# Two zero fills of the output moved behind the last token gather, with the expert weights one slot earlier

## The chip, the cores and the metric

The kernel runs on one core of a Trainium2 chip. The core has five engines: TensorE (PE: matmuls and weight loads), VectorE (DVE), ScalarE (ACT), GpSimd (POOL) and the sync engine (SP), which here only issues transfers. Transfers between DRAM and on-chip memory run on 16 DMA engines that all queues share: those that SP or ACT issue (queue q1 and q10 in the profile) and those that Pool issues (queue q0, which can also convert types and use indices). The metric is the device time of one execution in microseconds (us). The profile counts the span from the first to the last instruction, which is about 2 us shorter.

## The reference

Sparse attention is followed by a layer of experts with a capacity. There are 4 batches, 8 heads, 768 positions and 64 elements a head; 8 experts of 512 x 1024 x 512, each of which takes at most 80 tokens.

```python
# attention: each query keeps the 6 best chunks of 32 keys (by an upper bound), causal
ub = np.sum(np.maximum(q[..., None, :] * k_min[:, :, None], q[..., None, :] * k_max[:, :, None]), axis=-1)
top_chunks = np.argsort(np.where(causal, ub, -1e9), axis=-1)[..., -6:]
...
attn_out = softmax(masked scores) @ v
x = attn_out.transpose(0, 2, 1, 3).reshape(3072, 512)
# experts
logits = x @ w_gate;  expert_idx = argmax(logits);  gate_w = softmax(logits)[expert_idx]
out = np.zeros((3072, 512), dtype=np.float32)
for e in range(8):
    tok_idx = tokens of expert e, of which at most 80 with the largest gate_w
    h = np.maximum(x[tok_idx] @ w1[e], 0.0)
    out[tok_idx] = gate_w[tok_idx, None] * (h @ w2[e])
```

(The lines in words stand for code that is cut.) At most 640 of the 3072 rows of the output are not zero. So the kernel writes zeros over the whole output, 1536 KB for each of the four batches, and then scatters the rows of the experts into it. A row's scatter must come after the zeros of its batch, and since a round of rows may lie in any batch, each scatter waits for all four fills.

## The kernel before

The program is written with a helper, `op(engine, instruction, r=..., w=...)`. It works out from the names that an operation reads (`r`) and writes (`w`) which semaphores its engine must wait for. `sp` and `gpd` are transfers issued by SP and by Pool. Each engine runs its operations in program order.

The main loop runs over 16 pairs of heads, `i` = 0 to 15 (`NP` = 16); pair `i` belongs to batch `i // 4`. Weights are loaded meanwhile, one transfer of 1024 KB (as written, in bf16; the source is f32) at the end of a pair:

```python
def wload(e, part):          # part 0: w1 of expert e, part 1: w2
    ...
    op("gpd", lambda: gp.dma_start(w1s[e][:], src), w=[f"w1_{e}"], dsem=f"d_w1_{e}")
...
def fill(g, zs, zk):         # zeros over the output of batch g, from a zeroed tile
    zd = bass.AP(out.tensor, out.offset + g * NT * 128 * Dm, [[Dm, 128], [128 * Dm, NT], [1, Dm]])
    op("sp", lambda: sp.dma_start(zd, zs), r=[zk], w=[f"outz{g}"], dsem=f"d_zero{g}")

def last_w2(fbs):            # w2 of the last expert, in 8 pieces of 128 KB, into freed buffers
    for fb in fbs:
        ...
        op("gpd", lambda: gp.dma_start(w2f(E - 1, fb), src), ..., w=[f"w27{fb}"], dsem="d_w2_7")

for i in range(NP):
    ...
    if i == NP - 1:
        wload(E - 1, 0)
    folds(i, 0, 1)
    if i == NP - 1:
        last_w2(range(4))
    ...
    rows(i - 1); scale_rows(i - 1)        # writes the pair's rows to x_rows in DRAM (SP)
    ...                                   # at i == NP - 2: fill(3) from a cleared part of G
    if 0 < i < NP - 3:
        wload((i - 1) // 2, (i - 1) % 2)
    if i == NP - 2:
        wload(E - 2, 0)
        wload(E - 2, 1)
    if i in (0, 1, 12):                   # fills 0, 1, 2; the zeros lie in w1s[6], not loaded yet
        ...
        fill(min(i, 2), bass.AP(w1s[E - 2], ...), zk)
```

After the loop come the last pair's rows, the choice of tokens (`idx`, and per round the rows' places `idR` and weights `gR`), and the experts. A gather fetches an expert's tokens from `x_rows`, `turn` transposes them, `up` multiplies by w1 and applies Relu (first half on ACT, second half on DVE), and `down` multiplies by w2. There are six rounds of `down`, each over four groups of 32 rows. A round ends with an eviction on DVE, scaled, into one of four buffers `y`, and a scatter into the output:

```python
def gather(e):
    op("gpd", lambda: gp.indirect_dma_start(xgv(e), None, xd, ...),
        r=XD + ["idx"] + ([f"xS{e - 3}"] if e > 2 else []), w=[xgk(e)], dsem=f"d_g{e}")
...
def down(r):
    ...                                   # 32 matmuls into OB (the last round: 64, in two halves)
    op("dve", lambda: ve.tensor_scalar(yv(r)[:, c0:c1], o, gR[:, r:r + 1], None, ALU.mult),
       r=[k, "gR"], w=[f"y{r % 4}"] + k0)
    op("gpd", lambda: gp.indirect_dma_start(out, ..., yv(r), None, ...),
       r=[f"y{r % 4}", "idR"] + [f"outz{g}" for g in range(B)], w=[f"out{r}"], dsem=f"d_o{r % 4}")

for e in range(3):
    gather(e)
keep_warm(4); spread(); ...; keep_warm(12)       # idle matmuls while the gathers run
turn(0)
gather(3)
keep_warm(2)
up(0, lambda: turn(1, "dve"))
gather(4)
for e in range(1, E):
    if 1 < e + 1 < E:
        turn(e + 1)
        if e + 4 < E:
            gather(e + 4)
            if e + 4 == E - 1:
                last_w2(range(4, FB))
    up(e)
    if e % 4 > 0 and e != 3:
        down(e // 4 * 3 + e % 4 - 1)             # e = 1, 2, 5, 6, 7: rounds 0, 1, 3, 4, 5
    elif e == 4:
        down(2)
```

`xS{e - 3}` is the copy of the transposed tokens of expert e - 3, whose gather buffer is used again. Round 4 uses the buffer `y0` of round 0 again, and round 5 that of round 1.

Of the kernel before, what the change touches and what calls it, by code (L numbers as in the profile page):

```python
# [147 lines left out]
def bass_quest_chunk_select__then__topk_capacity_drop_kernel(  # L148
# [57 lines left out]
    with ExitStack() as pers:  # L206
# [17 lines left out]
        with nc.Block() as blk:  # L224

            @blk.sync
            def _body(_unused):
# [102 lines left out]
                def xgk(e):  # L330
                    return ("qn", "kn")[e % 2] + f"{e // 4}{e // 2 % 2}"
# [580 lines left out]
                    op("act", lambda: ac.activation(bass.AP({"q": qn, "k": kn}[n][s], 0, [[NT * 2 * D, CAP], [1, 512]]), zero, ACTF.Copy, scale=0.0),  # L912
                       r=[f"{n}n{s}{g}" for g in range(4)] + ["ident_f"], w=[f"{n}n{s}0", f"{n}n{s}1"])

                def fill(g, zs, zk):
                    zd = bass.AP(out.tensor, out.offset + g * NT * 128 * Dm, [[Dm, 128], [128 * Dm, NT], [1, Dm]])
                    op("sp", lambda: sp.dma_start(zd, zs), r=[zk], w=[f"outz{g}"], dsem=f"d_zero{g}")

                def last_w2(fbs):
                    for fb in fbs:  # L920
# [9 lines left out]
                for i in range(NP):  # L930
                    kk, bb = i % NPB, i // NPB - 1
                    live = bb >= 0
                    scores(i, 0, 2)
                    if i == NP - 1:
                        sort_rows(True)
                        vw_mm()
                        clear_xg("k", 0)
                    if i:
                        sums(i - 1)
                        scale_lg(i - 1)  # L940
                    if i == NP - 1:
                        wload(E - 1, 0)
                    folds(i, 0, 1)
                    if i == NP - 1:
                        last_w2(range(4))
                    if live and kk == 0:
                        gate_in(bb)
                    if live and kk == 1:
                        rank_pred()
                        rank_cmp(bb, 5)  # L950
                    scores(i, 2, 4)
                    if i == 0:
                        take_r(1)
                    if i == NP - 2:
                        op("act", lambda: ac.activation(G[:, 0:Dm], bass.AP(ident_f, 0, [[128, 128], [0, Dm]]), ACTF.Copy, scale=0.0),
                           r=["ident_f"], w=["growP"])
                    if live and kk == 2:
                        rank_count(bb)
                        rank_slot(bb)
                    if live and kk == 3 and i < NP - 1:  # L960
                        table(bb)
                        merge(bb)
                    if i == 12:
                        sort_apply()
                        sort_take()
                    if i:
                        if i == NP - 1:
                            sort_rank(0)
                        rows(i - 1)
                        scale_rows(i - 1)  # L970
                    if i == NP - 2:
                        fill(3, bass.AP(G, 0, [[2 * S, 128], [0, NT], [1, Dm]]), "growP")
                        rank_late(bb)
                    if live and kk == 0:
                        gate_exp()
                        gate(bb)
                    scores(i, 4, 6)
                    if i + 1 < NP:
                        bounds(i + 1)
                    if i + 2 < NP:  # L980
                        take_q(i + 2)
                        take_r(i + 2)
                    if i + 1 < NP:
                        bounds_out(i + 1)
                    if i + 2 < NP:
                        take_k(i + 2)
                    if i == 3:
                        op("dve", lambda: ve.tensor_scalar(triM[:], triQ[:], 1.0, 3e38, ALU.is_ge, ALU.mult), r=["triQ"], w=["triM"])
                        op("dve", lambda: ve.scalar_tensor_tensor(triM[:], ident_f[:], 3e38, triM[:], ALU.mult, ALU.max),
                           r=["triM", "ident_f"], w=["triM"])  # L990
                    if i + 4 < NP:
                        load(i + 4, "qk")
                    if i == NP - 4:
                        load_vk(NP - 1, 0)
                    if live and kk == 0:
                        rank_own(bb)
                    if live and kk == 1:
                        rank_diag(bb)
                        rank_cmp(bb, 4, 3, 2, 1, 0)
                    if live and kk == 2 and i < NP - 2:  # L1000
                        rank_late(bb)
                    if i == NP - 1:
                        sort_rank(1)
                        break
                    if i == NP - 2:
                        for n, s in (("q", 0), ("q", 1), ("k", 1)):
                            clear_xg(n, s)
                    values(i)
                    if i == NP - 2:
                        table(bb)  # L1010
                        merge(bb)
                        vw_turn()
                    if i + 2 < NP:
                        load(i + 2, "v")
                    if i + 1 < NP:
                        unselT(i + 1)
                    if live and kk == 0:
                        rank_row(bb)
                    if i == 11:
                        sort_rows(False)  # L1020
                        sort_rank()
                    if 0 < i < NP - 3:
                        wload((i - 1) // 2, (i - 1) % 2)
                    if i == NP - 2:
                        wload(E - 2, 0)
                        wload(E - 2, 1)
                    if i in (0, 1, 12):
                        zk = f"w1_{E - 2}"
                        zt = bass.AP(w1s[E - 2], 0, [[DB * Fd, 128], [1, 2 * Dm]]).bitcast(F32)
                        if i == 0:  # L1030
                            op("dve", lambda: ve.memset(zt, 0.0), w=[zk])
                        fill(min(i, 2), bass.AP(w1s[E - 2], 0, [[DB * Fd, 128], [0, NT], [1, 2 * Dm]]).bitcast(F32), zk)

                b = B - 1
                sums_last()
# [91 lines left out]
                def down(r):  # L1127
                    last = r == 5
                    groups = [(r // 3 * 4 + e, sb) for e, sb in ROUNDS[r % 3]]
                    o = OB[:, r % 2 * 512:r % 2 * 512 + Dm]  # L1130
                    parts = [(o, f"O{r % 2}", 0, Dm)]
                    if last:
                        n = Dm // 2
                        parts = [(o[:, 0:n], f"O{r % 2}", 0, n), (SC[0][:, 0:n], "SC0", n, Dm)]
                    for o, k, c0, c1 in parts:
                        for fb in range(FB):
                            for g, (e, sb) in enumerate(groups):
                                op("pe", lambda: pe.matmul(o[g * 32:g * 32 + 32, :], hTv(e)[:, fb * HW + sb * 32:fb * HW + sb * 32 + 32],  # L1138
                                                           w2f(e, fb)[:, c0:c1], start=(fb == 0), stop=(fb == FB - 1)),
                                   r=[f"hT{e % 4}{fb // 4}"] + ([f"w2_{e}"] if e < E - 1 else [f"w27{f}" for f in range(FB)]), w=[k], inc=(fb == FB - 1 and g == 3))  # L1140
                        k0 = ["E2", "E3", "E4", "E5"] if r == 0 else []
                        op("dve", lambda: ve.tensor_scalar(yv(r)[:, c0:c1], o, gR[:, r:r + 1], None, ALU.mult),
                           r=[k, "gR"], w=[f"y{r % 4}"] + k0)
                    op("gpd", lambda: gp.indirect_dma_start(
                        out, bass.IndirectOffsetOnAxis(ap=idR[:, r:r + 1], axis=0), yv(r), None,
                        bounds_check=NTOK - 1, oob_is_err=False), r=[f"y{r % 4}", "idR"] + [f"outz{g}" for g in range(B)], w=[f"out{r}"], dsem=f"d_o{r % 4}")

                for e in range(3):
                    gather(e)
                keep_warm(4)  # L1150
                spread()
                for e in range(4):
# [8 lines left out]
# [3 lines that stand above are left out]
                        if e + 4 < E:  # L1164
                            gather(e + 4)
                            if e + 4 == E - 1:
                                last_w2(range(4, FB))
                    up(e)
                    if e % 4 > 0 and e != 3:
                        down(e // 4 * 3 + e % 4 - 1)  # L1170
                    elif e == 4:
                        down(2)
# [36 lines left out]
```

## Time and profile before

| | |
|---|---|
| time, median of 3 runs | 290.12 us (290.0 to 290.32) |
| span of the profiled execution | 288.1 us |
| busy: PE, DVE, ACT, POOL | 274.3, 213.1, 147.0, 227.2 us |
| chain that ended last: PE, POOL, DVE, DMA | 70%, 15%, 6%, 4% of the span |
| three fills from `w1s`, one from `G` | 7.8 and 6.9 us from issue to landing (median of the page) |
| rows of a pair to `x_rows`, 16 transfers of 192 KB | 6.1 us median |
| w1 and w2 loads of 1024 KB | 9.8 and 11.2 us median |
| gathers, scatters | 2.6 us, 3.4 us median |

The page has the busy time of each engine, the span in 40 slices, the DMA queues, the chain of work that ended last (followed back from the last instruction through whatever released it), the costliest groups of instructions, and the transfers with their time from issue to landing. The trace behind it answers closer questions: single instructions in order of time, who waited for whom, and the share of the DMA engines in any stretch. A transfer's instruction on its queue is short; the transfer itself ends at its landing, when its semaphore is raised. A busy PE is no proof of progress, since the kernel also runs matmuls that only keep the array's clock up (`keep_warm`).

### The profile page before, as it was taken

To read this page: it belongs to the slowest core of one execution; us is meant where nothing else is said; L and a number is where in the kernel's file an instruction comes from. 1 tells how busy PE (TensorE), PEld (TensorE's weight loads), DVE (VectorE), ACT (ScalarE), POOL (GpSimd) and SP (SyncE) were. 2 spreads that over 40 slices of the span, in tenths; PEclk is the share of its full clock that TensorE was granted. 3 is DMA by queue.
4 is the path that set the end of the run, shared out by engine and by line. 5 is a ranking of instruction groups with operands and counts; after the bars stand their busy time and mean duration, and the time that the engine had idled before them with its cause. 6 is when DMAs were issued, how large, how long until landed. Compare 5 with 4: busy or idle time off the path is not lost.

```text
span 288.1 us, 8696 instructions
## 1 busy us (share of the span) xinstructions
PE 274.3 (95%) x3609; PEld 170.0 (59%) x3609; DVE 213.1 (74%) x575; ACT 147.0 (51%) x202; POOL 227.2 (79%) x295
## 2 busy tenths in 40 slices
PE   7899999999999999999999999999999999859991
PEld 7454656565656565656565656666656666428761
DVE  5897455566988989659889898898899888813341
ACT  2275656555576555555765555546756563403310
POOL 6079899998999999989999999899999970044732
PEclk9999999999999999999999999999999999998998
DMA  9999989999989999999999989995991599911361
GB/s 151 180 156 152 320 155 297 169 155 177 187 166 167 193 174 182 158 183 181 164 163 183 186 155 155 183 196 111 298 195 30 220 161 186 208 35 48 89 128 61
DMA packets 158359, 47.95 MB, mean 166 GB/s; under 512 B 142405, under 2 KB 150721, under 8 KB 158320
## 3 DMA queue, kind: packets, MB, share of 16 engines
q1 hardware_dynamic: 141664, 28.34, 50.9%
q0 software_dynamic: 13520, 18.67, 38.4%
q10 hardware_dynamic: 3136, 0.39, 0.9%
q8 instruction: 28, 0.46, 0.7%
q14 instruction: 11, 0.09, 0.1%
HBM read 53.49 MB, written 11.01 MB: 224 GB/s over the span
## 4 chain that ended last, share of the span: by engine, by line
PE 70%; POOL 15%; DVE 6%; DMA 4%; issue 2%; ACTq 1%; POOLq 0%; DVEq 0%
PE SC L509 22%; PE OB L568 19%; POOL ES L554 12%; PE SC L524 4%; PE M L595 4%; PE OB L1138 4%; PE SC L1114 4%; PE OB L641 3%; POOL EXB L545 3%; PE M L472 3%; DMA x_rows<-xp 2%; PE M L581 2%; PE MB L497 2%; DMA qn<-in_q_dram 1%; DMA qn<-x_rows,idx 1%
## 5 line engine op out<-in xcount | busy, mean ns | idle before, releaser
L531 ACT ACTIVATE EXB<-SC 128x1024 f32<-128x1024 f32 x96 | 86.2, 917 | 46.4 <-PE SC L524 45.1
L554 POOL TENSOR_TENSOR ES<-ES,EXB 128x256 f32<-128x256 f32 (+1 forms) x105 | 101.7, 980 | 4.8
L509 PE MATMUL SC<-qT,kT 64*128 64x512 f32 (+3 forms) x512 | 96.3, 466 | 0.1
L568 PE MATMUL OB<-EXB,vn 128*64 128x256 f32 (+3 forms) x704 | 72.8, 361 | 0.7 <-POOL EXB L545 0.7
L568 PEld LDWEIGHTS OB<-EXB,vn 128*64 128x64 f32 x704 | 46.9, 137 | 23.9 <-issue 9.8
L509 PEld LDWEIGHTS SC<-qT,kT 64*128 64x128 f32 x512 | 41.4, 186 | 23.0 <-issue 14.3
L554 POOL TENSOR_TENSOR ES<-EXB 128x768 f32<-128x768 f32 (+1 forms) x30 | 46.8, 1559 | 2.5
L524 PE MATMUL SC<-unsT,ind 64*128 64x128 bf16 (+5 forms) x256 | 37.7, 289 | 0.1
L576 ACT ACTIVATE oT<-OB 128x512 f32<-128x512 f32 (+1 forms) x32 | 15.6, 489 | 38.2 <-PE OB L568 38.2
L545 POOL TENSOR_SCALAR_AFFINE_SELECT EXB<-EXB 128x256 f32<-128x256 f32 x79 | 34.1, 442 | 0.0
L524 PEld LDWEIGHTS SC<-unsT,ind 64*128 64x128 bf16 x256 | 12.8, 95 | 17.9 <-issue 8.0
L439 DVE STREAM_TRANSPOSE qT<-qn 128x768 f32<-128x768 f32 x16 | 15.6, 974 | 7.2 <-PE SC L524 6.4
L586 DVE STREAM_TRANSPOSE M<-M 128x192 f32<-128x192 f32 x16 | 6.3, 394 | 19.2 <-PE M L595 18.9
L1091 POOL DMA_INDIRECT qn<-x_rows,idx x4 | 3.9, 987 | 20.8 <-DMA x_rows<-xp 19.0
L661 DVE TENSOR_TENSOR xp<-OB,rden 128x768 bf16<-128x768 f32 x16 | 15.3, 954 | 6.6 <-PE OB L641 6.3
L443 ACT ACTIVATE rq<-qT 128x768 f32<-128x768 f32 x16 | 13.5, 843 | 9.9 <-DVE qT L439 9.2
L449 DVE STREAM_TRANSPOSE kT<-kn 128x768 f32<-128x768 f32 x16 | 15.5, 966 | 1.2 <-DMA kn<-in_k_dram 1.2
L453 DVE TENSOR_REDUCE kmm<-kT 128x24 f32<-128x768 f32 x16 | 15.2, 950 | 0.5
L454 DVE TENSOR_REDUCE kmx<-kT 128x24 f32<-128x768 f32 x16 | 15.1, 942 | 0.0
L486 DVE MAX8 top<-M 128x8 f32<-128x8 f32 (+4 forms) x160 | 14.6, 164 | 0.6
L641 PE MATMUL OB<-ident_f,oT 128*128 128x128 f32 x96 | 13.9, 281 | 0.5 <-ACT oT L576 0.5
L456 POOL TENSOR_TENSOR kmm<-kmx,kmm 128x24 f32<-128x24 f32 x15 | 7.1, 471 | 9.2 <-DVE wg L907 9.2
(222 smaller groups left out, 415.6 us busy)
## 6 DMA issues: line engine op xcount, KB each, us to landing
w1s<-in_moe_w_dram POOLq DMA_DIRECT2D x8, 1024.0 KB, 9.8
w2s<-in_moe_w_dram POOLq DMA_DIRECT2D x7, 1024.0 KB, 11.2
vn<-in_v_dram SPq DMA_DIRECT2D x32, 192.0 KB, 4.8
kn<-in_k_dram SPq DMA_DIRECT2D x62, 96.0 KB, 2.7
qn<-in_q_dram SPq DMA_DIRECT2D x62, 96.0 KB, 3.1
out_dram<-w1s SPq DMA_DIRECT2D x3, 1536.0 KB, 7.8
x_rows<-xp SPq DMA_DIRECT2D x16, 192.0 KB, 6.1
out_dram<-G SPq DMA_DIRECT2D x1, 1536.0 KB, 6.9
```

The source lines that it names most:

```text
L439: op("dve", lambda: ve.transpose(qT[j][:], qn[s][:].rearrange("p a b c -> p (a b c)")), r=[f"qn{s}{g}" for g in range(4)], w=[f"qT{j}"])
L449: op("dve", lambda: ve.transpose(kT[j][:], kn[s][:].rearrange("p a b c -> p (a b c)")), r=[f"kn{s}{g}" for g in range(4)], w=[f"kT{j}"])
L453: op("dve", lambda: ve.tensor_reduce(kmm[j][:, 0, 0:NCH], kv, AX, ALU.min), r=[f"kT{j}"], w=[f"kmm{j}"])
L509: op("pe", lambda: pe.matmul(o, kT[j][pr, ts(kt)], qT[j][pr, q0:q1], start=True, stop=False), r=[f"kT{j}", f"qT{j}"], w=[f"SC{s}"], inc=False)
L524: op("pe", lambda: pe.matmul(o, ind[pr, ts(kt)], unsT[j][pr, b0 - 128:q1 - 128], start=False, stop=True), r=[f"ind{h}", f"unsT{j}"], w=[f" ...
L531: op("act", lambda: ac.activation(Ex(st, None, 0, W), src, ACTF.Exp, scale=SCALE), r=[f"SC{s}"], w=[f"E{st}"])
L545: op("gp", lambda: gp.affine_select(ad, a, pattern=[[0, 2], [1, 128]], compare_op=ALU.is_ge, fill=0.0, base=0, channel_multiplier=-1), r=[ ...
L554: op("gp", lambda: gp.tensor_tensor(o, in0, in1, ALU.add), r=[f"E{s2}", f"E{first[0]}"] if first else [f"E{s2}"] + kt, w=kt)
L568: op("pe", lambda: pe.matmul(OB[pr, q0:q1], vn[s][:, kt, h, :], ex, start=(n == 0), stop=last), r=[f"vn{s}{h}", "ES0" if st is None else f ...
L576: op("act", lambda: ac.activation(oT[:, q0:q1], OB[:, q0:q1], ACTF.Copy), r=[f"O{bk}"], w=[f"oT{bk}"])
L641: op("pe", lambda: pe.transpose(OB[:, ts(t)], oT[:, ts(t)], ident_f[:]), r=["oT0", "oT1", "ident_f"], w=[f"O{t // 4}"], inc=(t in (3, NT - ...
L661: op("dve", lambda: ve.tensor_tensor(xo, xi, rx, ALU.mult), r=["O0", "O1", "rden"], w=[f"xp{i % 2}"])
```

## The change

The fills of batches 2 and 3 leave the loop (pairs 12 and 14). They are issued by SP once the last gather has landed, from a part of `ES` that ACT has cleared. The scatters of rounds 0 and 1 follow in Pool's order behind the last gather and the last weight pieces; those of rounds 2 to 5 stand where they stood. Since the zeros in `w1s[6]` are no longer needed after pair 1, w1 of expert 6 can be loaded at pair 13, and w1 of expert 7 moves from pair 15 to the end of pair 14. The purpose is to take DMA traffic out of the end of the attention, where weights, fills and the rows of `x_rows` share the DMA engines, and to place it in the expert stage.

```diff
--- before.py
+++ after.py
@@ -912,9 +912,9 @@
                     op("act", lambda: ac.activation(bass.AP({"q": qn, "k": kn}[n][s], 0, [[NT * 2 * D, CAP], [1, 512]]), zero, ACTF.Copy, scale=0.0),
                        r=[f"{n}n{s}{g}" for g in range(4)] + ["ident_f"], w=[f"{n}n{s}0", f"{n}n{s}1"])
 
-                def fill(g, zs, zk):
+                def fill(g, zs, *zk):
                     zd = bass.AP(out.tensor, out.offset + g * NT * 128 * Dm, [[Dm, 128], [128 * Dm, NT], [1, Dm]])
-                    op("sp", lambda: sp.dma_start(zd, zs), r=[zk], w=[f"outz{g}"], dsem=f"d_zero{g}")
+                    op("sp", lambda: sp.dma_start(zd, zs), r=list(zk), w=[f"outz{g}"], dsem=f"d_zero{g}")
 
                 def last_w2(fbs):
                     for fb in fbs:
@@ -938,8 +938,6 @@
                     if i:
                         sums(i - 1)
                         scale_lg(i - 1)
-                    if i == NP - 1:
-                        wload(E - 1, 0)
                     folds(i, 0, 1)
                     if i == NP - 1:
                         last_w2(range(4))
@@ -951,9 +949,6 @@
                     scores(i, 2, 4)
                     if i == 0:
                         take_r(1)
-                    if i == NP - 2:
-                        op("act", lambda: ac.activation(G[:, 0:Dm], bass.AP(ident_f, 0, [[128, 128], [0, Dm]]), ACTF.Copy, scale=0.0),
-                           r=["ident_f"], w=["growP"])
                     if live and kk == 2:
                         rank_count(bb)
                         rank_slot(bb)
@@ -969,7 +964,6 @@
                         rows(i - 1)
                         scale_rows(i - 1)
                     if i == NP - 2:
-                        fill(3, bass.AP(G, 0, [[2 * S, 128], [0, NT], [1, Dm]]), "growP")
                         rank_late(bb)
                     if live and kk == 0:
                         gate_exp()
@@ -1019,17 +1013,17 @@
                     if i == 11:
                         sort_rows(False)
                         sort_rank()
-                    if 0 < i < NP - 3:
+                    if 0 < i < NP - 2:
                         wload((i - 1) // 2, (i - 1) % 2)
                     if i == NP - 2:
-                        wload(E - 2, 0)
                         wload(E - 2, 1)
-                    if i in (0, 1, 12):
+                        wload(E - 1, 0)
+                    if i in (0, 1):
                         zk = f"w1_{E - 2}"
                         zt = bass.AP(w1s[E - 2], 0, [[DB * Fd, 128], [1, 2 * Dm]]).bitcast(F32)
                         if i == 0:
                             op("dve", lambda: ve.memset(zt, 0.0), w=[zk])
-                        fill(min(i, 2), bass.AP(w1s[E - 2], 0, [[DB * Fd, 128], [0, NT], [1, 2 * Dm]]).bitcast(F32), zk)
+                        fill(i, bass.AP(w1s[E - 2], 0, [[DB * Fd, 128], [0, NT], [1, 2 * Dm]]).bitcast(F32), zk)
 
                 b = B - 1
                 sums_last()
@@ -1141,12 +1135,18 @@
                         k0 = ["E2", "E3", "E4", "E5"] if r == 0 else []
                         op("dve", lambda: ve.tensor_scalar(yv(r)[:, c0:c1], o, gR[:, r:r + 1], None, ALU.mult),
                            r=[k, "gR"], w=[f"y{r % 4}"] + k0)
+                    if r > 1:
+                        scatter(r)
+
+                def scatter(r):
                     op("gpd", lambda: gp.indirect_dma_start(
                         out, bass.IndirectOffsetOnAxis(ap=idR[:, r:r + 1], axis=0), yv(r), None,
                         bounds_check=NTOK - 1, oob_is_err=False), r=[f"y{r % 4}", "idR"] + [f"outz{g}" for g in range(B)], w=[f"out{r}"], dsem=f"d_o{r % 4}")
 
                 for e in range(3):
                     gather(e)
+                op("act", lambda: ac.activation(bass.AP(ES, 0, [[2 * S, 128], [1, Dm]]), bass.AP(ident_f, 0, [[128, 128], [0, Dm]]), ACTF.Copy, scale=0.0),
+                   r=["ident_f"], w=["zero", "D0", "U0", "D1", "L1", "U1"])
                 keep_warm(4)
                 spread()
                 for e in range(4):
@@ -1164,7 +1164,11 @@
                         if e + 4 < E:
                             gather(e + 4)
                             if e + 4 == E - 1:
+                                for g in (2, 3):
+                                    fill(g, bass.AP(ES, 0, [[2 * S, 128], [0, NT], [1, Dm]]), "zero", xgk(E - 1))
                                 last_w2(range(4, FB))
+                                for r in range(2):
+                                    scatter(r)
                     up(e)
                     if e % 4 > 0 and e != 3:
                         down(e // 4 * 3 + e % 4 - 1)
```

## The prediction

> **What bounds the kernel now.** I read the last 60 us only, since the change touches nothing earlier except one transfer near 201 us. First the chain of work that ended last, in order of time:
>
> ```profile
> 247.75 0.87 DVE xp L661
> ...
> 248.64 5.52 DMA x_rows<-xp
> ...
> 255.05 2.75 DMA qn<-x_rows,idx
> ...
> 258.17 0.83 PE SC L886 x2
> 259.00 1.07 PE SC L1114 x16
> ...
> 261.64 1.15 PE SC L1114 x32
> ...
> 282.39 0.50 DVE EXB L1142
> ```
>
> The columns are start, length, what. The last attention pair's rows go to DRAM (`x_rows`), and only when that write has landed may the first token gather run. From 258 us on the chain is TensorE alone, up to the last eviction and scatter. So two stretches set the end: the wait for `x_rows`, and the expert stage. Note that 16 matmuls of the first expert take 1.07 us and 32 of the next take 1.15: the first ran at half rate.
>
> Then the stretches (columns: window, its length, busy us of PE, PEld, DVE, ACT, POOL, TensorE clock, DMA share, GB/s):
>
> ```profile
> 216.00:220.00 4.00, 4.00 (x74) 2.66 (x72) 3.53 (x11) 2.52 (x3) 3.62 (x4) 1.00 0.01 2
> ...
> 236.00:241.00 5.00, 5.00 (x154) 3.79 (x152) 4.20 (x11) 1.30 (x2) 0.01 (x1) 1.00 1.16 187
> 241.00:248.60 7.60, 7.00 (x85) 4.45 (x82) 7.25 (x30) 5.44 (x10) 0.00 (x0) 1.00 1.16 201
> 248.60:254.20 5.60, 5.28 (x51) 2.35 (x50) 3.33 (x20) 0.00 (x0) 0.00 (x0) 1.00 0.85 151
> ...
> 258.00:270.60 12.60, 12.60 (x254) 9.85 (x255) 3.80 (x7) 4.38 (x10) 6.56 (x7) 0.86 0.20 58
> 270.60:278.90 8.30, 8.30 (x169) 5.13 (x170) 2.98 (x5) 1.75 (x4) 5.30 (x7) 1.00 0.66 126
> ```
>
> The DMA engines are idle at 216 to 220, full from 231 to 252, and nearly idle once the experts run. The change takes bytes out of the full stretch and puts others into the idle end.
>
> Third, the Pool timeline, where gathers, weight pieces and scatters share one queue:
>
> ```profile
> 267.62 0.98 POOL L1091 DMA_INDIRECT qn<-x_rows,idx  x1 [0.30 <-issue]
> 269.53 1.02 POOL L1144 DMA_INDIRECT out_dram<-EXB,idR  x1 [0.92 <-ACT kT L1123]
> 270.85 0.98 POOL L1091 DMA_INDIRECT kn<-x_rows,idx  x1 [0.30 <-issue]
> 271.83 0.64 POOL L922 DMA_DIRECT2D rq<-in_moe_w_dram  x1
> ```
>
> The last gather starts at 270.85, behind two scatters.
>
> Fourth, what one fill costs (the line that issues the fills, issue to landing):
>
> ```profile
> DMA to landing us min/median/max: 6.7/7.4/10.0
> ```
>
> **What the Trainium skill says.** "DMA: Bandwidth & Descriptors", section "Queues, rings and completion order": each DMA engine takes turns between its queues, packet by packet. The trace agrees: the `x_rows` write issued at 237.1 under the weight stream needed 12.2 us, the one at 220.9 on empty engines 2.9. The same page, "Anatomy of one DMA": about 2 us of a transfer is fixed, mostly the receipt of the write. Agrees: gathers of 80 KB take 2.5 to 2.8 us. "TensorE: Matmul & The Clock Gate", "What's actually happening": after an idle window of about 3.4 us the array runs at half clock until it has been busy for as long. Agrees: TensorE is idle from 254.73 to 257.85, and the clock record shows 0.50 for 3.4 us from 258.07.
>
> **Part 1: weights one slot forward, a fill gone from their path.** Today Pool issues three loads of 1024 KB and four of 128 KB between 229.8 and 235.1: 3.67 million bytes at about 0.2 million per us, done near 252.5. With w1 of expert 6 issued at 215.6 instead, into empty engines, 2.62 million stay. By the packet records 1.72 million have gone by 241; the other 0.9 million, at the 0.175 per us left beside the `x_rows` write of pair 14, end near 246.2. The last write, issued at 248.64, then meets empty engines: 2.9 us as at 220.9 in place of 5.52, landing at 251.5. The gather needs its indices as well, and VectorE finishes these at 251.37 + 0.16 = 251.53. So both meet, and no more can be had here. From landing to gather start is 0.9 us today (254.16 to 255.05), so the first gather starts at 252.4: **2.6 us gained**.
>
> The gap of TensorE shrinks with it. The warming matmuls end at 254.73; gather 0 lands at 252.4 + 2.75 = 255.2. A gap of 0.5 us should not drop the clock. Gathers 1 and 2 land 1.35 and 2.65 us later; the transposes of gather 2 run at 257.7 and expert 1 starts at 258.0, against 261.64: **3.6 us gained**, of which 1.0 is clock.
>
> The cost on Pool is one 0.77 us issue moved from 229.8 to 215.6. Pool waits 0.63 us for TensorE there today (215.61 to 216.25), so 0.15 us of delay is left, under 1 us of slack ahead of the next sums. The ACT clear of 0.62 us that goes had idle time around it. I count zero for these.
>
> **Part 2: two fills behind the last gather.** The two early scatters no longer stand ahead of gathers 6 and 7. Gather 7 now needs only the copy of transpose 4, which ended at 268.63; minus 3.6 it is 265.0, plus the 0.78 us that Pool took from release to start at gather 3: 265.8. It lands 2.65 later, 268.45, and releases the fills.
>
> In the packet records the fill of batch 3 has 768 packets of 2 KB from 223.37 to 227.73: 4.36 us, with engines full (86 ns a packet, over 16 engines). Two in a row: 1536 x 86 ns / 16 = 8.3 us. From issue to first packet I take 1.2 us (0.9 for the `x_rows` write at 220.9, 1.44 and 1.6 for other fills): 269.7. The four w2 pieces of expert 7 go out just ahead of them, 512 packets of 98 ns / 16 = 3.1 us, of which I guess half is done by then; 1.7 us still share the engines. Last packet: 269.7 + 8.3 + 1.7 = 279.7; with 0.5 us to the signal (227.73 to 228.2 at batch 3) the fills have **landed at 280.3**.
>
> Now the path behind. Scatter 0 starts 0.78 later (281.1) and lands in 2.7 to 4.8 us, median 3.4: 284.5. Round 4 writes the same y buffer as round 0 (four buffers), so its eviction on VectorE waits for that landing. Today it runs at 278.98, so it would be at 275.4 with part 1. It now runs at 284.6 to 285.3. Behind it in VectorE's order stands the second Relu of expert 7 (0.49), which ends at 285.9 against 280.72 today; TensorE's last 1.52 us (280.77 to 282.29) wait for that Relu. TensorE has been idle since about 277, so these run at half clock, by my guess 2.8 us: 288.7. From TensorE's end to the span's end today: 288.1 - 282.3 = 5.8. **Span 294.5**, against 288.1.
>
> As a ledger: -3.6 (part 1), +8.8 (Relu at 285.9 rather than 277.1), +1.3 (cold clock): +6.5. Beside 290.12 that is 296.6; I round down to **296.3**, since some of my landing times are medians of disturbed transfers.
>
> **Rivals.** *A: the fills are hidden.* Then -3.6 stands alone: 286.5, faster by 1.2%. For it: the DMA share of 0.20 to 0.66 in the expert stage, and 3 MB at some 390 GB/s are only 8 us. Against it: scatter 0 would have to land by 275.4, so the fills by about 271.3, which is 2.8 us after gather 7, and a single fill needs 6.7 at best. I give it 2%.
>
> *B: the fills wait, but the stall is shorter.* If the w2 pieces take no engine time from the fills, 1.7 us go; if scatter 0 lands in 2.7, another 0.7; if the clock stays up, 1.3. All together: 292.6. Any two of them bring the result within 2%.
>
> *C: the stall is longer.* If the clock drops after the attention all the same, part 1 is worth only 2.6: 297.3. If fills and weight pieces mix badly and the fills run at 300 GB/s, add 2.5. Pool must also issue six scatters in a row, 1.3 us each; the sixth could start at 281.1 + 6.5 = 287.6, before its data at 289.3, so Pool is not the bound.
>
> *D: the attention slows by Pool's moved issue.* At most +0.8; the idle 0.63 us speaks against it.
>
> **Range and chances.** B and C span 292.6 to 299.8 at their extremes; 8 times in 10 I expect 293.2 to 299.2. The line of +2% is 295.9, close below my centre. So slower by over 2% has 0.56, within 2% has 0.42, and faster by over 2% (under 284.3, which even A does not reach) 0.02.
>
> **What would show it.** Right: `x_rows` lands in about 2.9 us; first gather near 252.4; clock 1.00 at 258 to 261; last gather near 265.8 ahead of every scatter; two fills landing near 280; Pool idle some 10 us ahead of scatter 0; the eviction of round 4 waiting some 9 us for a scatter's landing; TensorE idle from 277 to 286. Wrong: fills landed by 272 (A); no wait of an eviction on a scatter; a first gather still near 255, which would mean that the weights were not what delayed `x_rows`; or a TensorE wait before 248 that is not there today (D).

## The result and the profile after

The changed kernel takes **297.46 us** (median of 4 runs, 297.03 to 298.32), the kernel before, run beside it, 290.06 us. The ratio is 1.026, 95% interval 1.023 to 1.029: slower by 2.6%. The span of the profiled execution grew from 288.1 to 295.3 us.

First the Pool timeline of the changed kernel, from the first gather on (start, length, operation; in brackets the idle time before it and what ended it):

```profile
252.65 1.05 POOL L1085 DMA_INDIRECT qn<-x_rows,idx  x1 [16.73 <-DVE idR L1076]
...
265.99 0.95 POOL L1085 DMA_INDIRECT kn<-x_rows,idx  x1 [2.30 <-ACT kT L1117]
...
282.62 1.03 POOL L1142 DMA_INDIRECT out_dram<-EXB,idR  x1 [13.43 <-DMA out_dram<-ES]
...
290.81 0.98 POOL L1142 DMA_INDIRECT out_dram<-EXB,idR  x1 [1.97 <-DVE EXB L1136]
```

The first gather starts at 252.65 where it started at 255.05, and what released it is VectorE's index work, no longer the rows. (By the program the gather needs `idx`, which ended at 251.66, 1.0 us before the start; the view names the last VectorE instruction before it, `idR`.) The last gather stands ahead of every scatter. Then Pool has nothing to do for 13.4 us, until the fills (`out_dram<-ES`) land.

Next the chain that ended last in the changed kernel, its end (start, length, what):

```profile
265.99 2.53 DMA kn<-x_rows,idx
...
268.96 12.75 DMA out_dram<-ES
...
282.62 2.74 DMA out_dram<-EXB,idR
...
285.46 0.75 DVE EXB L1136
286.21 0.41 DVE kT L1119
...
286.66 1.04 PE OB L1132 x13
287.70 1.73 PE SC L1132 x27
```

Before, this stretch of the chain was TensorE alone. Now it is one transfer after the other: last gather, fills, scatter 0. Only then come the eviction of round 4, the second Relu of expert 7 (`kT`) and the last matmuls. These matmuls took 1.5 us before and take 2.77 us now (286.66 to 289.43).

Third, stretches of the changed kernel (window, length, busy us of PE, PEld, DVE, ACT, POOL, TensorE clock, DMA share, GB/s):

```profile
248.70:252.60 3.90, 3.57 (x43) 1.56 (x42) 2.85 (x15) 0.59 (x1) 0.00 (x0) 1.00 0.24 51
...
258.00:270.60 12.60, 12.60 (x284) 9.19 (x287) 4.55 (x9) 4.37 (x10) 6.07 (x8) 1.00 0.31 57
268.50:281.70 13.20, 8.93 (x197) 6.06 (x189) 2.49 (x4) 2.19 (x5) 0.69 (x2) 0.95 0.92 279
281.70:290.00 8.30, 2.75 (x47) 1.72 (x47) 2.10 (x4) 0.00 (x0) 5.00 (x5) 0.50 0.33 127
```

The DMA share in the stretch of the last `x_rows` write fell from 0.85 to 0.24, so that part did what it was for. The full stretch is now 268.5 to 281.7, and it ends on the path. After it, TensorE works at half clock.

The waits of the changed kernel from 225 us on name the same two (us in total, times, longest):

```profile
POOL out_dram L1142 <- DMA out_dram<-ES: 13.4, 1, 13.4
...
DVE EXB L1136 <- DMA out_dram<-EXB,idR: 11.3, 1, 11.3
```

### The profile page after: what moved, and what is told of

Same layout as the page of the kernel before. It is cut to its first block, busy times and chain, and to the rows that moved or that the text cites. A ratio compares the mean times of both kernels' runs of the same rounds, so it can differ in the third digit from the quotient of the medians.

```text
span 295.3 us, 8696 instructions
## 1 busy us (share of the span) xinstructions
PE 275.2 (93%) x3609; PEld 170.1 (58%) x3609; DVE 213.1 (72%) x575; ACT 147.1 (50%) x202; POOL 226.8 (77%) x295
## 4 chain that ended last, share of the span: by engine, by line
PE 64%; POOL 16%; DMA 8%; DVE 7%; issue 2%; ACTq 1%; POOLq 0%; ACT 0%; SPq 0%; DVEq 0%
PE SC L509 21%; PE OB L568 18%; POOL ES L554 12%; DMA out_dram<-ES 4%; PE SC L524 4%; PE M L595 4%; PE OB L641 3%; POOL EXB L545 3%; PE M L472 2%; PE M L581 2%; PE OB L1132 2%; PE MB L497 2%; DMA qn<-in_q_dram 1%; PE SC L1108 1%; DMA out_dram<-EXB,idR 1%
## 5 line engine op out<-in xcount | busy, mean ns | idle before, releaser
L1142 POOL DMA_INDIRECT out_dram<-EXB,idR x6 | 6.0, 996 | 16.6 <-DMA out_dram<-ES 13.4
L1136 DVE TENSOR_SCALAR EXB<-OB,gR 128x512 f32<-128x512 f32 (+1 forms) x6 | 4.2, 706 | 17.9 <-DMA out_dram<-EXB,idR 11.3
## 6 DMA issues: line engine op xcount, KB each, us to landing
w2s<-in_moe_w_dram POOLq DMA_DIRECT2D x7, 1024.0 KB, 10.5
```

## The experiments

My theory: the two parts are independent. The weights one slot forward gain some 3 us, because the last write of rows meets empty DMA engines. The late fills cost some 10 us, because every scatter waits for them, and because the eviction of round 4 waits for scatter 0. Rivals: the gain comes from the fills' absence; the loss comes from the reuse of four buffers alone, from the clock, or from the w2 pieces beside the fills. The experiments ran in three groups, each beside the kernel before. Its time differs from group to group (290.02, 289.61 and 291.51 us), so ratios are compared; differences in us between kernels of different groups are good to about 1 us at best. Executions more than 1.5% above the fastest of their kernel (4 of 12 for the fills behind gather 3, at most 2 of any other kernel in a group) are left out of the medians.

### Part 1 alone

Only the `wload` lines of the change; fills and scatters stay where they were.

```diff
-                    if i == NP - 1:
-                        wload(E - 1, 0)
-                    if 0 < i < NP - 3:
+                    if 0 < i < NP - 2:
                         wload((i - 1) // 2, (i - 1) % 2)
                     if i == NP - 2:
-                        wload(E - 2, 0)
                         wload(E - 2, 1)
+                        wload(E - 1, 0)
```

> Part 1 alone: the weights one slot forward, all four fills and all scatters where they were before. My theory (the full DMA stretch at the end of the attention delays the last write of rows, and the expert stage starts 3.6 us late because of it): the write lands in 2.2 to 2.9 us, the first gather starts near 252.6, expert 1 near 258.1, and the time falls by 3.4 us, to 286.7. Rival (the gain needs the fill of batch 3 out of the way, or gathers 6 and 7 ahead of the scatters): less than half of it, 288.5 or more.

Measured: 287.22 us, ratio 0.989 (0.985 to 0.993). The gain is there without moving a single fill, so the rival falls. It is 2.8 us here; the repetition below gives 3.3. The interval of each is about 1 us to either side.

### Part 2 alone

The changed kernel with the weights put back to their old slots (the diff above reversed).

> Part 2 alone: the two fills behind the last gather, the weights as before. My theory (the two parts add up, and the fills alone cost what the change loses plus what part 1 gains): the last write of rows again lands in about 5.5 us, the first gather starts near 255, the fills land near 285, the time is 297.5 + 3.4 = 300.9. Rival (the fills were what crowded the rows, so that moving them gives the gain): the first gather starts near 252.6 and the time is 297.5.

Measured: 300.74 us, ratio 1.036 (1.030 to 1.043). From the chain of this kernel:

```profile
248.78 5.34 DMA x_rows<-xp
...
255.00 2.62 DMA qn<-x_rows,idx
...
272.25 12.47 DMA out_dram<-ES
```

The write of rows is as slow as before (5.34 us), the gather starts at 255.00 as before, and the fills end at 284.7. The parts add up: -2.8 (part 1) and +10.7 (part 2) make 7.9; the change as a whole made 7.4, which is the same within the intervals.

### Six y buffers

```diff
-                    return bass.AP(EXB, 2048 + (r % 4) * 512, [[EXP, 128], [1, Dm]])
+                    return bass.AP(EXB, 2048 + r * 512, [[EXP, 128], [1, Dm]])
...
-                           r=[k, "gR"], w=[f"y{r % 4}"] + k0)
+                           r=[k, "gR"], w=[f"y{r}"] + k0)
```

(and the scatter reads `y{r}`). Rounds 4 and 5 then wait for no scatter.

> The changed kernel with six y buffers in place of four, so that rounds 4 and 5 wait for no scatter. If the reuse of the buffer is what costs the time, the stall of VectorE and TensorE goes and the end comes with it: 288 or less. My theory: the stall goes and TensorE ends near 279, but all six scatters still wait for the fills to land at 281.7 and then leave Pool one after another, 1.3 us apart; the last starts at 282.6 + 5 x 1.3 = 289.1 in place of 290.8, so 1.7 us are gained: 295.8.

Measured: 295.43 us, ratio 1.018 (1.013 to 1.023), 2.0 us below the changed kernel (2.4 by the ratios). VectorE's last eviction, in this kernel's timeline, and the row of scatters on Pool:

```profile
279.08 0.48 DVE L1136 TENSOR_SCALAR EXB<-SC,gR 128x256 f32<-128x256 f32 x1 [0.39 <-PE SC L1132]
```

```profile
283.31 1.03 POOL L1142 DMA_INDIRECT out_dram<-EXB,idR  x1 [13.95 <-DMA out_dram<-ES]
...
289.82 0.98 POOL L1142 DMA_INDIRECT out_dram<-EXB,idR  x1 [0.30 <-issue]
```

All results are ready at 279.6, and nothing can leave. The stall of TensorE and VectorE that fills the changed kernel's profile for 9 us is thus worth some 2 us: behind it stands the landing of the fills, followed by six scatters 1.3 us apart.

### One fill behind the last gather

```diff
-                                for g in (2, 3):
+                                for g in (3,):
...
-                    if i in (0, 1):
+                    if i in (0, 1, 12):
```

The fill of batch 2 is back at pair 12.

> The changed kernel with one fill behind the last gather (batch 3); that of batch 2 is back at pair 12. My theory (the end follows the landing of the last fill one to one): the fill lands about 4 us earlier, near 277.5, and the time falls by 4, to 293.4. Rival (the cost is the wait itself or the place of the scatters, not the bytes): 296.5 or more.

Measured: 293.18 us, ratio 1.012 (1.010 to 1.016), 4.3 us below the changed kernel (3.9 by the ratios). The chain of this kernel has the single fill at

```profile
268.59 9.06 DMA out_dram<-ES
```

which ends at 277.65 in place of 281.71: 4.1 us. The end follows the landing of the last fill one to one, as far as these numbers can tell.

### TensorE kept busy during the stall

```diff
                     up(e)
+                    if e == E - 1:
+                        keep_warm(40)
```

> The changed kernel with 40 warming matmuls (8.6 us) behind the last expert's w1 product, where TensorE is idle while VectorE waits for scatter 0. My theory (TensorE's last stretch takes 2.8 us in place of 1.5 because the clock has fallen): it takes 1.5 to 1.6 us, and the time falls by 1.2, to 296.2. Rival (the stretch is long because of its own waits): no change, 297.5.

Measured: 296.31 us, ratio 1.022 (1.019 to 1.025), some 1.2 us below the changed kernel. The two intervals overlap, so the times alone do not show the gain; the profile does. The stretch with the last 47 matmuls, first in the changed kernel, then in this one:

```profile
286.60:289.50 2.90, 2.75 (x47) 1.72 (x47) 0.49 (x2) 0.00 (x0) 1.93 (x2) 0.50 0.42 164
```

```profile
287.80:290.00 2.20, 1.49 (x47) 1.19 (x47) 0.97 (x2) 0.00 (x0) 1.90 (x2) 1.00 0.50 194
```

The same matmuls take 2.75 us at clock 0.50 and 1.49 us at 1.00. In this profile the fills happened to land later (282.90 for 281.71), so the spans are alike (295.2 and 295.3 us); from the landing to the end it is 12.3 us in place of 13.6. The clock's share of the loss is about 1.2 us.

### The gap ahead of the experts, filled

The kernel before, with `keep_warm(25)` in place of `keep_warm(12)`.

> The kernel before with 25 warming matmuls in place of 12 ahead of the first transposes: they fill the gap of TensorE (254.7 to 257.85) and change no transfer. My theory (1.0 us of the 3.6 us gained ahead of expert 1 is the clock, which falls to half after this gap): the clock stays at 1.00 in 258 to 261.5, expert 1 starts 1.0 us earlier, 289.1. Rival (the first expert waits for gathers 1 and 2, not for the clock): no change, 290.1.

Measured: 289.11 us against 289.61, ratio 0.998 (0.997 to 0.999): half of what I expected. Its profile, though, shows the whole of it. First the kernel before, then this one:

```profile
258.00:261.50 3.50, 3.50 (x47) 2.91 (x45) 0.39 (x2) 0.88 (x2) 1.64 (x3) 0.51 0.24 61
```

```profile
258.00:261.50 3.50, 3.08 (x73) 2.60 (x72) 0.81 (x2) 1.60 (x4) 2.50 (x3) 1.00 0.23 67
```

73 matmuls in place of 47 in the same 3.5 us, and every scatter 1.1 us earlier than in the profile before (265.20 to 266.29 at the first). Of the 26 executions of the kernel before that were compared here, 5 had a mean granted clock of 0.994 or 0.995, with a median of 288.72 us, and 21 had 0.985 to 0.991, with 289.69. By this grouping the fallen clock costs 1.0 us, and it falls in four executions of five. That does not explain the small gain, for the median of all 26, 289.61, is nearly that of the 21. With 25 warming matmuls no execution had a clock under 0.994, and yet their median is 0.4 us above that of the 5. What takes these 0.4 us stays open; the interval of the gain, 0.2 to 1.0 us, holds the 0.8 that four executions of five would give.

### The w2 pieces ahead of the fills

```diff
                             gather(e + 4)
+                            if e + 4 == E - 2:
+                                last_w2(range(4, FB))
                             if e + 4 == E - 1:
...
-                                last_w2(range(4, FB))
```

> The changed kernel with the last four w2 pieces of expert 7 issued behind gather 6 in place of gather 7, so that their bytes have moved before the fills start. My theory (the pieces take DMA time from the fills): the fills start at once and land 2 us earlier, about 10.5 us after issue, and the time falls by about 2, to 295.5. Rival (the pieces end before they matter, and the fills are bound by their own writes): 297.3.

Measured: 304.38 us, ratio 1.051 (1.047 to 1.054): a miss by 9 us. The chain of this kernel says why:

```profile
265.36 4.64 DMA unsT<-in_moe_w_dram
...
270.08 0.45 ACT kT L1117
...
278.88 10.77 DMA out_dram<-ES
```

My edit made a new wait. `last_w2` is recorded as a reader of `kT0`, and the Relu of expert 2, which writes `kT0`, came after it in the program, so that Relu waited for the pieces (8.1 us in the waits of this kernel). The fills themselves landed 10.8 us after issue in place of 12.75. I repeated it with the pieces recorded behind that Relu:

```diff
                     up(e)
+                    if e == 2:
+                        last_w2(range(4, FB))
```

> As the last run, mended: the four w2 pieces are issued behind gather 6, but recorded after the Relu of expert 2, so that this Relu no longer waits for them. My theory (the pieces take DMA time from the fills; in the run before, the fills landed 10.8 us after issue in place of 12.7, and its 7 us of loss came from the Relu's wait alone): no wait of ACT for the pieces, gather 7 starts near 266.1 to 266.3, the fills land 10.8 us after issue, near 279.6, and the time falls by 2.0 to 295.5. Rival (the pieces cost the path elsewhere too, say through a later gather 7): 297.0 or more.

Measured: 298.31 us against 291.51, ratio 1.024 (1.020 to 1.027). This lies within the interval of the changed kernel, so a gain is not shown, and my 2 us are a miss. From the chain of this kernel:

```profile
267.62 3.48 DMA kn<-x_rows,idx
...
271.54 11.09 DMA out_dram<-ES
```

The fills need 1.7 us less (11.09 for 12.75), but the last gather, now behind the pieces, needs 0.95 more (3.48 for 2.53), and it releases them. That leaves 0.7 us, which is also the difference of the two ratios (1.0236 and 1.0261). Stretches of this kernel, from the first packet of the fills on, show why no more came of it:

```profile
272.03:280.20 8.17, 6.77 (x149) 4.49 (x141) 1.53 (x3) 1.31 (x3) 0.00 (x0) 1.00 1.02 376
280.20:282.20 2.00, 0.00 (x0) 0.00 (x0) 0.00 (x0) 0.00 (x0) 0.00 (x0) 1.00 0.14 45
```

The engines are full for 8.2 us, and then the last packets trickle out for 2 us at a DMA share of 0.14. By the packet records the fills run for 10.1 us from first packet to last here, 9.9 in the run before, and 10.5 in the changed kernel. So clearing the pieces away brought the first packet forward (0.9 us after the issue in place of 2.4) and shortened the run itself by only 0.3 to 0.6 us.

### The fills earlier in the expert stage

The fills released by gather 3 in place of gather 7:

```diff
                 gather(3)
+                for g in (2, 3):
+                    fill(g, bass.AP(ES, 0, [[2 * S, 128], [0, NT], [1, Dm]]), "zero", xgk(3))
                 keep_warm(2)
```

> The changed kernel with the two fills released by the landing of gather 3 (about 259.5) in place of gather 7 (268.5). My theory (the fills cost time only because they land after scatter 0 is due, near 272): they land about 12.7 us or less after 259.5, near 271, scatter 0 starts about when Pool has issued the last weight pieces, nothing waits, and the gain of part 1 remains: 286.7, give or take 0.7. Rival (fills beside gathers 4 to 7 delay these, and TensorE waits for them): 288 to 291.

Measured: 288.24 us, ratio 0.994 (0.991 to 0.996): 9.2 us below the changed kernel, but 1.0 us above part 1 alone in the same group. So the loss is indeed a matter of when the fills land, and most of it goes with an earlier release: by the ratios about nine tenths here and seven in the repetition. But the fills are not free. To see why, I ran it again, and also with all gathers sent at once:

```diff
-                        r=XD + ["idx"] + ([f"xS{e - 3}"] if e > 2 else []), w=[xgk(e)], dsem=f"d_g{e}")
+                        r=XD + ["idx"], w=[xgk(e)], dsem=f"d_g{e}")
```

> The fills released by gather 3 once more, for another profile. I expect 288.2 again: gather 6 lands some 6 to 8 us after its issue, TensorE waits about 2 us for it, and nothing else waits for the fills by more than 0.5 us. Rival: gather 6 lands in 3 us and the 1 us over the weights alone comes from Pool's row of scatters at the end.

> The fills released by the landing of gather 3, and gathers 3 to 7 no longer held back by the copies of earlier experts (each has a buffer of its own): all eight leave Pool 1.3 us apart, the last at about 261.7. My theory (with the fills behind gather 3 alone, a gather issued while the fills run lands up to 7.8 us after issue and TensorE waits some 2 us for it): all gathers land well before they are needed, the fills land near 272, scatter 0 lands near 275 when the eviction of round 4 is due, and the time is that of the weights alone, 287.2, give or take 0.7. Rival (the bytes of two fills can't be hidden in the expert stage at all): 288.2 or more.

> Part 1 alone once more, beside the two others on the same chip: 2.8 us below the kernel before (ratio 0.989 to 0.991), and the lowest of the four; gather 0 starts about 1 us after the indices, whatever the clock does.

Measured in one group, beside the kernel before at 291.51 us: part 1 alone 288.23, ratio 0.988 (0.986 to 0.991); the fills behind gather 3 291.04, ratio 1.000 (0.997 to 1.002); the same with all gathers at once 294.94, ratio 1.011 (1.008 to 1.013). Part 1 alone is the lowest, as expected. The other two miss: 288.2 and 287.2 were expected.

In the profile of the fills behind gather 3, the gathers' time to landing (of the four whose landing the trace has), then the weight loads' wait for gather 6, then TensorE's longest waits from 252 to 284 us (total, times, longest):

```profile
DMA to landing us min/median/max: 2.5/5.4/7.3
```

```profile
271.99 0.18 PEld L1094 LDWEIGHTS MB<-ident_bf,qn 80*128 80x128 bf16 x4 [1.59 <-DMA qn<-x_rows,idx]
```

```profile
PE OB L1132 <- DVE qT L1119: 2.0, 2, 1.2
PE MB L1094 <- DMA qn<-x_rows,idx: 1.6, 2, 1.1
```

A gather of 80 KB issued while the fills run lands after up to 7.3 us in place of 2.6. TensorE's weight loads wait 1.6 us for gather 6 and its matmuls 1.1. That is the smaller part of the loss: this profile's span is 3.9 us above that of part 1 alone (290.3 and 286.4). TensorE also waits 2.0 us, in two pieces, for VectorE's Relu (`qT`), and VectorE in turn had stood still: the second of these Relus began at 276.17, 2.7 us after the last record of the matmuls that it reads (273.45), and the trace does not tell what released it.

With all gathers at once no matmul waits more than 0.5 us for a gather, and yet that kernel is 6.7 us slower than part 1 alone. Its TensorE waits, from 252 to 284 us, are

```profile
PE SC L1108 <- issue: 3.5, 7, 1.1
PE MB L1094 <- DMA qn<-x_rows,idx: 0.7, 2, 0.5
```

Six of the seven gaps, 3.2 us in all, lie in the midst of the 32 matmuls of expert 1, between 259.3 and 264.0, nearly all of them while the fills' packets run (260.0 to 270.0). TensorE waited there for nothing that the profile shows. VectorE and ScalarE stood still as well (5.35 and 5.98 us), until about 6 us after the last record of the matmuls that they read. The clock then fell to half from 262.1 to 268.9. As an estimate, the 3.2 us of gaps and half of the 5.6 us for which TensorE was busy at half clock make up 6.0 of the 6.7 us. What TensorE lacked stays open. One 16 KB transfer of the instruction queue in that stretch took 1.54 us, so a late supply of instructions is possible, but no run shows it; in the kernel before two such transfers took 1.72 and 1.80 us without gaps like these.

## Why the prediction was right, and where its sizes were off

The direction, the mechanism and the range held: 296.3 was predicted, 297.46 measured, 293.2 to 299.2 the range. That the loss exceeds 2% had been given only 0.56, and some of the closeness is luck, since errors cancelled. By its steps:

- **Part 1: the write of rows.** Right in kind, better in size. The write landed 2.2 us after its issue (I took 2.9), at 251.0, although the weight stream ended 2.7 us later than worked out: its last packet was done at 248.9 instead of 246.2, and the write was issued at 248.76. (The 3.67 million bytes that the prediction has done near 252.5 fit its 0.175 million per us, not its 0.2.) The sum left room that was not there, and the write only just met empty engines. The indices alone now release the gather, and it started at 252.65 (252.4 predicted). Parts 1 and 2 alone show that the weights, not the fills, did this.
- **Part 1: the clock.** Expert 1 started at 258.23 (258.0). The clock stayed at 1.00. What I had not seen is that the kernel before pays this 1.0 us in most executions only. Part 1 alone gave 2.8 and 3.3 us of the 3.6 predicted, which the intervals do not tell apart from it. The prediction also calls a window of 3.4 us confirmed by the trace, but the idle time that it names, 254.73 to 257.85, is 3.1 us.
- **Moved Pool issue.** Zero, as counted: the first fold behind it started at 216.54 in place of 216.25, and the last `x_rows` write was issued 0.12 us later than before.
- **Gather 7.** 265.99 to 268.53 (265.8 to 268.45).
- **The fills: the term that was mis-sized.** I had 11.9 us from the gather's landing to theirs; it was 13.2, and they landed at 281.71 instead of 280.3. The packets of 2 KB were as costly as taken (84 ns for 86). But the first of them came 2.4 us after the issue, not 1.2; with the w2 pieces out of the way it came after 0.9 us (both runs with earlier pieces). From first packet to last I had 10.0 us, and it was 10.5, but the two parts of that sum are wrong in opposite ways: with the pieces gone the fills still took 9.9 to 10.1 us, not 8.3, and the pieces' share was 0.3 to 0.6 us, not 1.7. So the pieces cost the fills mainly their start. What the 8.3 left out is the end, when few packets are left and most engines are idle.
- **Scatter 0.** 2.74 us to landing, where I took the median of 3.4; by luck, this made up half of the error above. The eviction of round 4 began at 285.46 (284.6), the Relu ended at 286.6 (285.9), TensorE ended at 289.43 (288.7).
- **Cold clock.** 2.77 us for the last matmuls (2.8 guessed), and the run with warming matmuls confirms it: the same matmuls then took 1.49.
- **Rival A** (fills hidden) fell; **B** found no two of its three reliefs: scatter 0 was quick, the pieces and the clock were not. Of **C**, the clock held after the attention, and the fills were late by 1.4 us where it allowed 2.5. Its remark that Pool's row of six scatters is not the bound holds only while the buffers are reused; with six buffers it is the bound. **D** fell.

One thing the working did not say: the wait that it followed step by step, of the eviction on scatter 0, is worth only some 2 us. Without it the end would have been set by the fills' landing and Pool's six scatters all the same.

## What to carry to other kernels

A transfer of filler bytes is free only while its landing is early enough for the first work that depends on it: work the landing out from bytes, rate and what else is queued (here 3 MB, 13 us), and compare it with that moment, not with the end of the kernel. A quiet DMA share in the last stage is not room by itself, for small gathers on the path share the same engines and took up to 7.3 us in place of 2.6; and TensorE and VectorE then stood still for longer than those gathers explain, for a reason that stays open. When a change joins two moves, run each alone: here the weights one slot forward gave 0.989 on their own, and the other half, 1.036 on its own, lost more than three times as much.

## What the runs showed of the hardware that was not expected

- The fills' 2 KB packets took 84 ns each (median) on 16 engines, about 390 GB/s while all were busy. The weight pieces that convert f32 to bf16 took 98 ns for 1 KB as written. A piece of weights so takes more than twice the DMA time of the same bytes of zeros.
- That rate does not give the landing: 3.1 MB of fills took 9.9 to 10.5 us from first packet to last, and about the last 2 us ran at a DMA share of 0.14 to 0.39.
- Two fills issued behind four such pieces sent their first packet 2.4 us after the issue; with the pieces gone, after 0.9 us.
- After a gap of 3.1 us on TensorE, 21 of 26 executions have a mean clock that fits a stretch at half clock, and 5 do not.
- With two fills and all gathers in flight, TensorE stood still six times amid matmuls that wait for nothing recorded, up to 1.1 us each. The cause is open.
